# Closing loads of `wo` recut, two closing copies moved to ScalarE, and the load of `x` issued later

## The chip, the cores and the metric

The kernel runs on one core of a Trainium2 chip. A core has a matrix engine (TensorE, called PE in the profile, with its weight loads shown apart as PEld), three engines for element-wise work (VectorE, called DVE; ScalarE, called ACT; GpSimd, called POOL) and SyncE (SP), which here only issues transfers. Sixteen DMA engines carry data between HBM, the chip's large memory, and SBUF, the core's working memory. TensorE writes its results into PSUM, a small memory of eight banks, from which VectorE and ScalarE copy them out. The engines run at the same time and wait for one another through semaphores.

The metric is the device time of one execution in microseconds (us). A median of several executions is given, and beside it one further execution was taken by the hardware profiler; that one has a time of its own, and all durations of single instructions come from it.

## What is computed

One token (a row `x` of 1024 numbers) goes through an attention block and a two-layer MLP, and the results are added to `x`:

```python
xn = layernorm(x)
# attention on layernorm'ed x; 32 query heads, 4 key/value heads, last 4096 positions of the caches
q  = (xn @ wq) as 32 heads of 128
p  = softmax(q @ k.T * 128**-0.5)          # k, v: [4 heads, 4096, 128]
a  = (p @ v as 4096 numbers) @ wo          # wo: [4096, 1024]
# MLP on layernorm(xn)
h  = gelu(layernorm(xn) @ w1 + b1)         # w1: [1024, 3584]
m  = h @ w2 + b2                           # w2: [3584, 1024]
out = x + a + m                            # 1024 numbers
```

All inputs and the output are bf16. The weights and the used part of the caches are some 40 MB, each number of which is used once.

## The kernel before

The kernel is straight-line code: every instruction is written out in order for each engine, and waits on semaphores are set by hand. Each engine does its own list strictly in order.

**Loads.** All the large transfers go through SP's queue, in this order: `wq` (8 MB, into the SBUF buffer `WA`), two loads of keys (into `KT`), `w1` (7 MB, into `W1`), two loads of values (into `V`), then `w2` (7 MB, again into `WA`, issued once the product with `wq` is done, L298), then `wo` (8 MB, issued once the product with `w1` is done, L382 to L387). The weights are laid out so that each of the 128 partitions takes a run of consecutive rows; the 4096 rows of `wo` are 32 rows (of 1024 numbers, 2 KB) on each partition. The helper `load_rows` (L148) issues one transfer for each entry of a list of row counts, and each transfer has a semaphore of its own. `WO_CHUNKS` (L29) is that list for `wo`. Its first three entries, 28 rows, go into `W1`, whose weights have been used by then; the rest goes into `KT`, whose keys have been used by then.

ScalarE issues the three small loads: `x` and `b1` (L169, L170) after a wait for VectorE's third memset (`C["qbz"]`, L165), and `b2` (L245) after the first transpose of `x` (L241).

**GpSimd** builds constants from the start on: a matrix of ones, an identity, the selection matrix `SELQ` (L181 to L186, whose end is called `C["selq"]`), then masks and further selection matrices. SP's key loads wait for `C["selq"]` (L187).

**The front of the work.** `x` lands, VectorE transposes it (L241), then come sums on TensorE (L252), a square root on ScalarE (L256), and the normalised `XNTb` (L260); a second norm gives `YTb` (L277). TensorE waits for `wq` and multiplies (L289, name `"q"`). The keys are transposed on VectorE (L331), TensorE makes the scores (L345), softmax follows (L352 to L380), then the product with `w1` (L289 again, name `"h"`), the product with the values (L427), the GELU (L391 to L413, result `GT`) and the attention output `OT` (L448).

**The closing product.** The products with `w2` and with the first 28 rows of `wo` (`WO_BULK`, L30) go to one PSUM bank, bank 6: for each row two matmuls of 512 columns (`bulk`, L457 to L461), which leave one result row on partition 0 and one on partition 32. The last four rows of `wo` take another form: four matmuls of 256 columns each (L482), which leave their results in bank 7 on partitions 0, 32, 64 and 96, in the layout in which the output leaves. TensorE waits for the semaphore of each transfer of `wo` before its rows (L473). When the last of the 28 rows is done (`C["bulk"]`), VectorE copies the two result rows as four pieces of 256 numbers into `BULK` (L489 to L492), in that same layout. It then waits for the last matmul (`C["fin"]`), adds bank 7 and `BULK` (L495), and SP stores the result (L497).

Of the kernel before, what the change touches and what calls it, by code (L numbers as in the profile page):

```python
# [6 lines left out]
ACTF = mybir.ActivationFunctionType  # L7
AX = mybir.AxisListType

D = 1024  # L10
# [15 lines left out]
WQ_CHUNKS = [8]  # L26
W1_CHUNKS = [8]
W2_CHUNKS = [28]
WO_CHUNKS = [16, 8, 4, 2, 1, 1]  # L29
WO_BULK = 28  # L30


class Track:
# [11 lines left out]
def bass_parallel_sum__sliding_block_cached__mixer_channel_mlp__decode_kernel(  # L45
# [18 lines left out]
    pe, dve, act, pool, sp = nc.tensor, nc.vector, nc.scalar, nc.gpsimd, nc.sync  # L64

    def sems(name, n):
        return [nc.alloc_semaphore(f"{name}{i}") for i in range(n)]

    s_x, s_b1, s_b2, s_out = (nc.alloc_semaphore(n) for n in ("s_x", "s_b1", "s_b2", "s_out"))
# [3 lines left out]
    s_v = sems("s_v", NP)  # L73
    s_wo = sems("s_wo", len(WO_CHUNKS))
    s_w2 = sems("s_w2", len(W2_CHUNKS))

    PE = Track(nc, "S_PE")
    DVE = Track(nc, "S_DVE")
    ACT = Track(nc, "S_ACT")
    POOL = Track(nc, "S_POOL")  # L80

    def sb(name, shape, d):
        return nc.alloc_sbuf_tensor(name, shape, d)
# [3 lines left out]
    W1 = sb("W1", [128, KC * F], bf16)  # L87
    KT = sb("KT", [128, HKV * W], bf16)
# [7 lines left out]
    XB4 = sb("XB4", [128, 256], bf16)  # L96
    XT32 = sb("XT32", [128, 256], bf16)
    B1R = sb("B1R", [128, QW], bf16)
# [29 lines left out]
    OT = sb("OT", [128, 32], bf16)  # L128
    BULK = sb("BULK", [128, 256], f32)
    ORow = sb("ORow", [128, 256], bf16)  # L130
    PS = nc.alloc_psum_tensor("PS", [128, 8 * 512], f32)

    def bank(b, lo=0, n=512):
        return PS[:, b * 512 + lo: b * 512 + lo + n]

    x_rows = A_x.rearrange("b s (a n) -> (b s a) n", a=4)
    b2_rows = B_b2.rearrange("(a n) -> a n", a=4)
    b1_rows = B_b1.rearrange("(a n) -> a n", a=4)
# [3 lines left out]
    wo_p = A_wo.rearrange("(p j) n -> p j n", j=32)  # L142
    out_rows = out.rearrange("b s (a n) -> (b s a) n", a=4)

    C = {}


    def load_rows(dst, src, chunks, width, semaphores, first=0, c0=0, off=0):  # L148
        for j, n in enumerate(chunks):
            sp.dma_start(  # L150
                dst[:, off + c0 * width: off + (c0 + n) * width].rearrange("p (c n) -> p c n", c=n),
                src[:, first + c0: first + c0 + n, :],
            ).then_inc(semaphores[j], 16)
            c0 += n

    load_rows(WA, wq_p, WQ_CHUNKS, NQ, s_wq)
    def d(ins):
        return DVE.mark(ins)

    def dw():  # L160
        dve.wait_ge(DVE.sem, DVE.cnt)
# [2 lines left out]
    C["b1z"] = d(dve.memset(B1R[:, :], 0.0))  # L164
    C["qbz"] = d(dve.memset(QB[:, :], 0.0))  # L165

    with nc.allow_non_contiguous_dma(reason="small loads"):
        act.wait_ge(DVE.sem, C["qbz"])
        act.dma_start(XB4[0:128:32, :], x_rows).then_inc(s_x, 16)  # L169
        act.dma_start(B1R[0:128:32, :], b1_rows).then_inc(s_b1, 16)  # L170

    def p(ins):
        n = POOL.mark(ins)
        pool.wait_ge(POOL.sem, n)
        return n
# [6 lines left out]
    for q in range(4):  # L182
        ap = SELQ[32 * q:32 * q + 32, q * 128:(q + 1) * 128].rearrange("p (a j) -> p a j", a=4)
        p(pool.affine_select(out=ap, in_=ap, pattern=[[0, 4], [-1, 32]], compare_op=ALU.not_equal,
                             fill=1.0, base=0, channel_multiplier=1))
    C["selq"] = POOL.cnt  # L186
    sp.wait_ge(POOL.sem, C["selq"])  # L187
    for G in range(NP):
        sp.dma_start(
# [120 lines left out]
    for a in range(4):  # L310
        last = pe.matmul(bank(6, 16 + 32 * a, 32), lhsT=SELQ[:, a * 128:(a + 1) * 128], rhs=TQ[:, 0:1024:32],  # L311
                         start=True, stop=True)
# [14 lines left out]
    for G in range(NP):  # L327
        dve.wait_ge(s_k[G], 16)
        for h in range(2):
            lo = G * PW + h * W  # L330
# [8 lines left out]
    for G in range(NP):  # L339
        kg = KT[:, G * PW:(G + 1) * PW].rearrange("p (b c i) -> p c b i", b=PB, c=4)  # L340
        for nb in range(4):
            if nb % 2 == 0:
                pe.wait_ge(DVE.sem, C["kt"][2 * G + nb // 2])
            for c in range(4):
                last = pe.matmul(bank(nb), lhsT=QB[:, G * 512 + c * 128:G * 512 + (c + 1) * 128],  # L345
                                 rhs=kg[:, c, 16 * nb:16 * nb + 16, :], start=False,
                                 stop=(G == NP - 1 and c == 3))
# [29 lines left out]
        out=LR[:, :],  # L377
        in_=PS[0:1, 2 * 512 + 192:2 * 512 + 320].rearrange("o (a m) -> o m a", a=4), axis=AX.X, op=ALU.add))
    dw()
    C["rr"] = d(dve.reciprocal(  # L380
        out=RR4[:, :].rearrange("o (q m) -> o q m", q=4), in_=LR[:, :].unsqueeze(1).to_broadcast([1, 4, 32])))
# [1 line left out]

    wide_product(W1, W1_CHUNKS, F, s_w1, YTb, QW // 2, [4, 5], "h")
    sp.wait_ge(PE.sem, C["h"])
    load_rows(W1, wo_p, WO_CHUNKS[:3], D, s_wo[:3])
    load_rows(KT, wo_p, WO_CHUNKS[3:], D, s_wo[3:], first=WO_BULK)  # L387

    dve.wait_ge(PE.sem, C["h"])
    dve.wait_ge(s_b1, 16)  # L390
# [1 line left out]
        out=HW32[:, :].rearrange("p (b n) -> p b n", b=2),  # L392
# [32 lines left out]
    for t in range(32):  # L425
        q = t % 2
        last = pe.matmul(PS[64 * q:64 * q + 64, 3 * 512:4 * 512], lhsT=PT[:, t * 64:(t + 1) * 64], rhs=vb[:, t],  # L427
                         start=(t < 2), stop=(t >= 30))
# [7 lines left out]
        out=OM[:, :].rearrange("p (g d) -> p g d", g=HKV), in0=bank(3).rearrange("p (g d) -> p g d", g=HKV),  # L436
# [6 lines left out]
    for dq in range(4):  # L443
        last = pe.matmul(bank(2, 352, 32), lhsT=E4[:, dq * 128:(dq + 1) * 128],  # L444
                         rhs=ON[:, dq * 32:(dq + 1) * 32], start=(dq == 0), stop=(dq == 3))
# [11 lines left out]
    def bulk(weights, vec, c, lo, first, last):  # L457
        for q in range(2):
            ins = pe.matmul(PS[32 * q:32 * q + 1, 6 * 512:7 * 512], lhsT=vec[:, c:c + 1],  # L459
                            rhs=weights[:, lo + q * 512: lo + (q + 1) * 512], start=first, stop=last)  # L460
        return ins  # L461

    pe.wait_ge(DVE.sem, C["GT"])
    c = 0
# [6 lines left out]
    c = 0  # L471
    for j, n in enumerate(WO_CHUNKS):
        pe.wait_ge(s_wo[j], 16)  # L473
        for _ in range(n):
            if c < WO_BULK:
                last = bulk(W1, OT, c, c * D, False, c == WO_BULK - 1)
                if c == WO_BULK - 1:
                    C["bulk"] = PE.mark(last)
            else:
                for a in range(4):  # L480
                    lo = (c - WO_BULK) * D + a * 256
                    last = pe.matmul(PS[32 * a:32 * a + 32, 7 * 512:7 * 512 + 256],  # L482
                                     lhsT=OT[:, c:c + 1].to_broadcast([128, 32]), rhs=KT[:, lo:lo + 256],
                                     start=False, stop=(c == 31))
            c += 1
    C["fin"] = PE.mark(last)

    dve.wait_ge(PE.sem, C["bulk"])
    for a in range(4):  # L489
        q = a // 2  # L490
        lo = 6 * 512 + (a % 2) * 256
        d(dve.tensor_copy(BULK[32 * a:32 * a + 1, :], PS[32 * q:32 * q + 1, lo:lo + 256]))  # L492
    dw()
    dve.wait_ge(PE.sem, C["fin"])
    C["out"] = d(dve.tensor_tensor(out=ORow[:, :], in0=bank(7, 0, 256), in1=BULK[:, :], op=ALU.add))  # L495
# [33 lines left out]
```

## Time and profile before

| | |
|---|---|
| median of 3 runs | 101.97 us (101.0 to 102.63) |
| the profiled execution's own time | 100.91 us |
| its span, first to last instruction | 99.6 us |
| mean granted TensorE clock in it | 0.846 |
| TensorE busy | 48.4 us (49%), weight loads 19.3 us |
| VectorE busy | 38.8 us (39%) |
| ScalarE busy | 6.6 us (7%) |
| GpSimd busy | 9.6 us (10%) |
| read from HBM | 39.86 MB, 400 GB/s over the span |

The span is what the instructions show; 1.31 us of the profiled execution's time lie outside it. In the groups of the page, a line reads: line of the kernel, engine, operation, what it writes and reads, shapes and count, then busy time, mean duration in ns, and the idle time before it with the engine or transfer that ended it. In the timeline the two numbers ahead of a line are its start and its length in us. "SPq" and "ACTq" are the parts of SP and ScalarE that issue transfers. The row "PEclk" gives the granted clock of TensorE in tenths, the row "DMA" the busy share of the sixteen DMA engines in tenths, each over 40 equal slices of the span. The trace behind the page also holds a record of each DMA packet: queue, start, duration and bytes.

### The profile page before, as it was taken

What the parts mean: (1) busy time and instruction counts of PE and PEld (TensorE: products, weight loads), DVE (VectorE), ACT (ScalarE), POOL (GpSimd) and SP (SyncE); (2) the same over time, 40 slices, a digit from 0 to 9 for tenths busy, and PEclk for the clock granted to TensorE, in tenths of its full rate; (3) what the DMA queues carried; (4) which work ended last, traced back from release to release, by engine and by line L of the source; (5) the groups of instructions that cost most, each with busy time, mean ns of one, the idle gap of its engine ahead of it and who ended that gap; (6) DMA issues with size and microseconds to landing.
All of it is one profiled execution on the core that took longest, in us unless ns stands there. A gap on an engine that the chain in (4) does not pass through costs nothing.

```text
span 99.6 us, 859 instructions
## 1 busy us (share of the span) xinstructions
PE 48.4 (49%) x350; PEld 19.3 (19%) x350; DVE 38.8 (39%) x50; ACT 6.6 (7%) x11; POOL 9.6 (10%) x40
## 2 busy tenths in 40 slices
PE   0000220008973419756071179990800899795760
PEld 0000220003321003112020133540700223241210
DVE  4000443000027999999918175498100000000052
ACT  0000236000022000000000620000000000000000
POOL 5777720000000000000000000000000000000000
PEclk9999999999999555599999755999555558999999
DMA  9199999939999889998699999999889999999920
GB/s 421 79 474 553 423 474 474 447 132 428 428 441 651 368 368 391 529 529 375 253 428 428 434 510 414 483 553 391 368 368 431 421 414 421 414 424 390 382 100 1
DMA packets 1906, 39.89 MB, mean 400 GB/s; under 512 B 224, under 2 KB 240, under 8 KB 624
## 3 DMA queue, kind: packets, MB, share of 16 engines
q1 hardware_dynamic: 1880, 39.85, 93.9%
q8 instruction: 2, 0.03, 0.1%
q10 hardware_dynamic: 24, 0.01, 0.0%
HBM read 39.86 MB, written 0.00 MB: 400 GB/s over the span
## 4 chain that ended last, share of the span: by engine, by line
DMA 52%; DVE 25%; PE 17%; ACT 2%; issue 1%; SPq 0%; DVEq 0%
DMA W<-in_A_wo_dram 30%; DMA WA<-in_A_wq_dram 22%; DVE KT L331 17%; PE PS L289 12%; DVE MX L352 2%; ACT WA L367 2%; PE PS L345 2%; DVE BULK L492 2%; DVE TQ L307 1%; PE PS L459 1%; DVE Q L302 1%; DVE QB L322 1%; SPq L150 0%; DVE ORow L495 0%; PE PS L311 0%
## 5 line engine op out<-in xcount | busy, mean ns | idle before, releaser
L331 DVE STREAM_TRANSPOSE KT<-KT 128x4096 bf16<-128x4096 bf16 x4 | 17.4, 4412 | 0.0
L345 PE MATMUL PS<-KT,QB 128*128 128x512 bf16 x32 | 9.7, 459 | 8.7 <-DVE KT L331 8.7
L459 PE MATMUL PS<-WA,GT 128*1 128x512 bf16 x56 | 9.0, 498 | 5.1 <-DMA WA<-in_B_w_dram 5.1
L492 DVE COPY BULK<-PS 1x256 f32<-1x256 f32 x4 | 1.7, 417 | 23.4 <-PE PS L459 23.3
L289 PE MATMUL PS<-WA,XNTb 128*32 128x512 bf16 x64 | 6.5, 592 | 7.9 <-DMA WA<-in_A_wq_dram 7.9
L459 PE MATMUL PS<-W,OT 128*1 128x512 bf16 x56 | 6.5, 378 | 2.5 <-DMA W<-in_A_wo_dram 2.5
L252 PE MATMUL PS<-XT,onesf 128*128 128x16 f32 x2 | 0.6, 386 | 11.7 <-DVE XT L249 11.7
L345 PEld LDWEIGHTS PS<-KT,QB 128*128 128x128 bf16 x32 | 3.3, 112 | 15.6 <-DVE KT L331 11.5
L302 DVE CAST Q<-PS 128x512 bf16<-128x512 f32 x1 | 0.7, 692 | 13.1 <-PE PS L289 13.1
L289 PE MATMUL PS<-W,YTb 128*32 128x448 bf16 x64 | 5.4, 525 | 0.0
L459 PEld LDWEIGHTS PS<-WA,GT 128*1 128x1 bf16 x56 | 2.9, 104 | 10.9 <-issue 9.3
L289 PEld LDWEIGHTS PS<-WA,XNTb 128*32 128x32 bf16 x64 | 2.4, 142 | 11.6 <-DMA WA<-in_A_wq_dram 8.0
L241 DVE STREAM_TRANSPOSE XT<-XB 128x256 bf16<-128x256 bf16 x1 | 0.6, 625 | 8.5 <-DMA XB<-in_A_x_dram 8.5
L427 PE MATMUL PS<-V,WA 128*64 128x512 bf16 x32 | 3.6, 380 | 0.0
L459 PEld LDWEIGHTS PS<-W,OT 128*1 128x1 bf16 x56 | 2.2, 83 | 6.9 <-DMA W<-in_A_wo_dram 2.8
L367 ACT ACTIVATE WA<-PS,NMB 128x2048 bf16<-128x2048 f32 x1 | 2.0, 1967 | 23.3 <-DVE NMB L365 23.3
L444 PE MATMUL PS<-ON,E 128*128 128x32 f32 x8 | 1.9, 404 | 2.8 <-DVE ON L439 2.8
L370 DVE STREAM_TRANSPOSE WA<-WA 128x2048 bf16<-128x2048 bf16 x1 | 2.3, 2312 | 2.1 <-ACT WA L367 2.1
L352 DVE TENSOR_REDUCE MX<-PS 128x1 f32<-128x2048 f32 x1 | 2.3, 2291 | 2.0 <-PE PS L345 2.0
L289 PEld LDWEIGHTS PS<-W,YTb 128*32 128x32 bf16 x64 | 2.2, 138 | 3.0 <-issue 2.8
L252 PEld LDWEIGHTS PS<-XT,onesf 128*128 128x128 f32 x2 | 0.5, 312 | 11.7 <-DVE XT L249 11.7
L215 POOL TENSOR_SCALAR_AFFINE_SELECT E<-E 32x512 f32<-32x512 f32 x4 | 2.5, 629 | 0.6
(87 smaller groups left out, 37.3 us busy)
## 6 DMA issues: line engine op xcount, KB each, us to landing
W<-in_B_w_dram SPq DMA_DIRECT2D x1, 7168.0 KB, 45.2
WA<-in_B_w_dram SPq DMA_DIRECT2D x1, 7168.0 KB, 48.1
KT<-in_A_k_cache_dram SPq DMA_DIRECT2D x2, 2048.0 KB, 25.6
V<-in_A_v_cache_dram SPq DMA_DIRECT2D x2, 2048.0 KB, 51.6
W<-in_A_wo_dram SPq DMA_DIRECT2D x1, 4096.0 KB, 23.5
W<-in_A_wo_dram SPq DMA_DIRECT2D x1, 2048.0 KB, 28.0
W<-in_A_wo_dram SPq DMA_DIRECT2D x1, 1024.0 KB, 30.0
KT<-in_A_wo_dram SPq DMA_DIRECT2D x1, 512.0 KB, 30.8
```

Of the source, the lines that this page charges most:

```text
L215: p(pool.affine_select(out=ap, in_=ap, pattern=[[1, 4], [-1, 128]], compare_op=ALU.not_equal, fill=1.0, base=0, channel_multiplier=4))
L289: last = pe.matmul(PS[32 * a:32 * a + 32, banks[b] * 512: banks[b] * 512 + n], lhsT=vec[:, k:k + 1].to_broadcast([128, 32]), rhs=weights[: ...
L302: d(dve.tensor_copy(Q4[:, 0:512], bank(4)))
L331: C["kt"].append(d(dve.transpose(KT[:, lo:lo + W], KT[:, lo:lo + W])))
L345: last = pe.matmul(bank(nb), lhsT=QB[:, G * 512 + c * 128:G * 512 + (c + 1) * 128], rhs=kg[:, c, 16 * nb:16 * nb + 16, :], start=False, st ...
L352: C["mx"] = d(dve.tensor_reduce(out=MX[:, :], in_=PS[:, 0:2048], axis=AX.X, op=ALU.max))
L367: C["exp"] = ACT.mark(act.activation(out=Pb, in_=PS[:, 0:2048], func=ACTF.Exp, bias=NMB[:, 0:1], scale=SCALE, accum_out=RS[:, 0:1]))
L370: C["PT"] = d(dve.transpose(PT, Pb))
L427: last = pe.matmul(PS[64 * q:64 * q + 64, 3 * 512:4 * 512], lhsT=PT[:, t * 64:(t + 1) * 64], rhs=vb[:, t], start=(t < 2), stop=(t >= 30))
L444: last = pe.matmul(bank(2, 352, 32), lhsT=E4[:, dq * 128:(dq + 1) * 128], rhs=ON[:, dq * 32:(dq + 1) * 32], start=(dq == 0), stop=(dq == 3))
L459: ins = pe.matmul(PS[32 * q:32 * q + 1, 6 * 512:7 * 512], lhsT=vec[:, c:c + 1], rhs=weights[:, lo + q * 512: lo + (q + 1) * 512], start=fi ...
L492: d(dve.tensor_copy(BULK[32 * a:32 * a + 1, :], PS[32 * q:32 * q + 1, lo:lo + 256]))
```

## The change

Three things are changed.

1. `wo` is loaded in five transfers of 16, 9, 4, 2 and 1 rows in place of six of 16, 8, 4, 2, 1 and 1. The first two (25 rows, `WO_W1`) go into `W1`, the last three into `KT`. `WO_BULK` is 29 in place of 28: one more row takes the two matmuls of 512 columns, one fewer the four of 256.
2. Of the four closing copies, VectorE keeps the two from partition 0 and ScalarE takes the two from partition 32. VectorE gets a wait for ScalarE's second copy ahead of the closing addition.
3. ScalarE's issue of `x` and `b1` is moved behind GpSimd's `SELQ` in the code and waits for `C["selq"]` as well as for `C["qbz"]`.

```diff
-WO_CHUNKS = [16, 8, 4, 2, 1, 1]
-WO_BULK = 28
+WO_CHUNKS = [16, 9, 4, 2, 1]
+WO_BULK = 29
+WO_W1 = 25
...
-    with nc.allow_non_contiguous_dma(reason="small loads"):
-        act.wait_ge(DVE.sem, C["qbz"])
-        act.dma_start(XB4[0:128:32, :], x_rows).then_inc(s_x, 16)
-        act.dma_start(B1R[0:128:32, :], b1_rows).then_inc(s_b1, 16)
...
     C["selq"] = POOL.cnt
+    with nc.allow_non_contiguous_dma(reason="small loads"):
+        act.wait_ge(POOL.sem, C["selq"])
+        act.wait_ge(DVE.sem, C["qbz"])
+        act.dma_start(XB4[0:128:32, :], x_rows).then_inc(s_x, 16)
+        act.dma_start(B1R[0:128:32, :], b1_rows).then_inc(s_b1, 16)
     sp.wait_ge(POOL.sem, C["selq"])
...
-    load_rows(W1, wo_p, WO_CHUNKS[:3], D, s_wo[:3])
-    load_rows(KT, wo_p, WO_CHUNKS[3:], D, s_wo[3:], first=WO_BULK)
+    load_rows(W1, wo_p, WO_CHUNKS[:2], D, s_wo[:2])
+    load_rows(KT, wo_p, WO_CHUNKS[2:], D, s_wo[2:], first=WO_W1)
...
             if c < WO_BULK:
-                last = bulk(W1, OT, c, c * D, False, c == WO_BULK - 1)
+                last = bulk(W1 if c < WO_W1 else KT, OT, c, (c if c < WO_W1 else c - WO_W1) * D, False,
+                            c == WO_BULK - 1)
...
-                    lo = (c - WO_BULK) * D + a * 256
+                    lo = (c - WO_W1) * D + a * 256
...
     dve.wait_ge(PE.sem, C["bulk"])
+    act.wait_ge(PE.sem, C["bulk"])
     for a in range(4):
         q = a // 2
         lo = 6 * 512 + (a % 2) * 256
-        d(dve.tensor_copy(BULK[32 * a:32 * a + 1, :], PS[32 * q:32 * q + 1, lo:lo + 256]))
+        if q == 0:
+            d(dve.tensor_copy(BULK[32 * a:32 * a + 1, :], PS[32 * q:32 * q + 1, lo:lo + 256]))
+        else:
+            C["bulk_a"] = ACT.mark(act.activation(out=BULK[32 * a:32 * a + 1, :],
+                                                  in_=PS[32 * q:32 * q + 1, lo:lo + 256], func=ACTF.Copy))
+    dve.wait_ge(ACT.sem, C["bulk_a"])
     dw()
     dve.wait_ge(PE.sem, C["fin"])
```

## The prediction

> **What bounds the kernel now.** I read the page first, for the share of the DMA engines and the queues:
>
> ```profile
> DMA  9199999939999889998699999999889999999920
> ...
> q8 instruction: 2, 0.03, 0.1%
> ```
>
> Transfers fill the span. The low digits (1, 3) are long packets booked in one slice; in the packet records the engines follow packet on packet from 1.82 us to 96.56 us. So a step ahead of 95 us counts only if it delays the issue of a transfer past its turn. The last such issues, those of `wo`, are over at 66.35 us, and the first packet of `wo` starts at 74.99: it stood in line. Only the head and the tail are free to move. So the tail, in the chain of work that ended last:
>
> ```profile
> 94.58 1.05 PE PS L459 x8
> ...
> 96.99 0.42 DVE BULK L492
> ...
> 97.45 0.04 issue
> 97.49 0.42 DVE ORow L495
> ```
>
> Four copies (95.65 to 97.41) release the addition. Beside them the timeline has the last row of `wo`:
>
> ```profile
> 97.07 0.29 PE L482 MATMUL PS<-KT,OT 128*32 128x256 bf16 x4 [0.33 <-DMA KT<-in_A_wo_dram]
> ```
>
> It ends at 97.36, so with 0.04 of issue the addition could start at 97.40: the copies hold it up by 0.09 us. Then busy shares by stretch; the last but one number is that of the DMA engines:
>
> ```profile
> 95.00:95.50 0.50, 0.50 (x6) 0.09 (x2) 0.00 (x0) 0.00 (x0) 0.00 (x0) 1.00 0.39 143
> 95.50:96.00 0.50, 0.26 (x10) 0.12 (x8) 0.35 (x1) 0.00 (x0) 0.00 (x0) 1.00 0.14 53
> ```
>
> At the end 0.14 is busy: two engines of sixteen. The packet records name the cause: the two "instruction" packets of q8 (46.52 to 47.51, 81.36 to 82.38) each held one engine for 1.0 us, and these two have been last at every landing since.
>
> **1. The loads of `wo`.** The bytes stay. Each engine serves 8 partitions: 8 packets per load and a closing one. Packet records: 2 KB 0.084 us, 4 KB 0.159, 8 KB 0.311, 16 KB 0.611, 32 KB 1.215, closing 0.009. Between 16 and 32 KB a further 2 KB cost 0.075, so the new 18 KB packet should take 0.686. Before: 8 x (1.215 + 0.611 + 0.311 + 0.159 + 2 x 0.084) = 19.71. After: 8 x (1.215 + 0.686 + 0.311 + 0.159 + 0.084) = 19.64. With one closing packet fewer: -0.08 us. Bounds: 0, and +0.6 if the 18 KB packets ran at the 2 KB packets' rate (0.041 ns per byte against 0.037, on 8 x 18432 bytes); I take the interpolation, because 56 KB packets, no power of two either, took 2.12 us, the same 0.037. SP's issue of one load (0.43 us) goes too, far ahead of its turn: nothing.
>
> The last matmuls then run from 97.07 - 0.08 = 96.99 to 97.28. Back from there by the old spacings (0.62 for one row, 1.27 for two), the four-row load, which now closes bank 6, frees TensorE at 95.10; eight matmuls take 1.05 as before, so bank 6 is done at 96.15 (before: 95.63). The nine rows ahead need 2.1 us (their 16 matmuls took 1.89) from about 92.65 on and are out of the way. That one row changes from the narrow to the wide form is hidden in TensorE's waits for `wo`.
>
> **2. The copies.** VectorE keeps two: from 96.17, 0.41 + 0.03 + 0.41, to 97.02. A copy of 1x256 by ScalarE is not in the trace. Nearest: 0.27 us (32x128) and 0.60 (128x512); by columns 256 lies at 0.38, which I take. Two end at about 96.96, beside VectorE's. Both are done before 97.28, so the new wait, behind which only the addition stands, costs nothing. At 0.27 nothing changes; at 0.60 ScalarE ends at 97.40, the addition starts at 97.46, and 0.03 is left of the gain. A table load (1.28 us at L273) would add another 0.8; but the Copy at L304 ran behind that load and the Exp at L367 behind a Copy, both without a further load, so it is left out.
>
> TensorE's last row then sets the addition: 97.28 + 0.04 = 97.32 in place of 97.49, **-0.17 us**. Late next is that landing itself; addition, store and its landing (2.1 us) only move along.
>
> **3. The issue of `x`.** The timeline:
>
> ```profile
> 2.14 1.07 ACTq L169 DMA_DIRECT2D XB<-in_A_x_dram  x1
> 2.53 1.64 POOL L184 TENSOR_SCALAR_AFFINE_SELECT SELQ<-SELQ 32x128 bf16<-32x128 bf16 x4
> ...
> 10.61 0.62 DVE L241 STREAM_TRANSPOSE XT<-XB 128x256 bf16<-128x256 bf16 x1 [8.50 <-DMA XB<-in_A_x_dram]
> ...
> 22.81 6.46 PE L289 MATMUL PS<-WA,XNTb 128*32 128x512 bf16 x64 [7.93 <-DMA WA<-in_A_wq_dram]
> ```
>
> `SELQ` ends at 4.17, so `x` (1.07) and `b1` (0.51) are issued some 2.05 us later, beside SP's issues (4.19 to 7.34). In the records the packets of `x` take turns with those of `wq`: 7.3 to 7.8, and their closing packets one `wq` packet (2.44) later, at 9.8 to 10.3. Later by 2.05 means one turn later: `x` lands at 13.0 instead of 10.6. Behind the waiting ScalarE stand `b1`, then `b2`, the table load and the square root; VectorE and TensorE wait for them. `XNTb` comes at 16.3 instead of 13.82; the product waits for `wq` until 22.81. Cover: 8.96 us. If `x` kept to the very last turn of `wq`, it landed by 22.7 and the product began 3.2 us late; that too is covered, by TensorE's 5.07 us of waiting for `w2` at 77.5. `b1` is read at 63.65, `b2` at 72.07. SP's loads only join a line that lasts to 21.6. So nothing is lost. A gain is bounded by the head: `wq`'s first sixteen packets took 3.05 us in the mean, the next ones 2.45, while `x` was being issued. If the issue of `x` were the cause, 0.6 would come back; a first packet must also fill the path, so I take 0 and keep -0.6 for the range.
>
> **Sum.** 100.91 - 0.17 = 100.74 for the profiled execution. The median of the runs lies 1.06 above it, so 101.97 - 0.17 = **101.8 us**. What a measurement of this kernel tells from no change is about 2%: 99.9 to 104.0.
>
> **Rivals.**
>
> *Slower: TensorE's clock falls in the tail.* The granted clock changes in steps of 3.41 us. Stretches of one step, PE's busy time first, then PEld, DVE, ACT, POOL, clock:
>
> ```profile
> 28.58:31.99 3.41, 1.25 (x18) 0.43 (x11) 2.07 (x3) 0.73 (x2) 0.00 (x0) 1.00 1.42 610
> 42.23:45.64 3.41, 1.42 (x8) 0.46 (x6) 3.41 (x2) 0.00 (x0) 0.00 (x0) 1.00 1.16 504
> 66.12:69.54 3.42, 1.35 (x14) 0.46 (x10) 2.89 (x10) 0.23 (x1) 0.00 (x0) 1.00 1.24 537
> 90.87:94.28 3.41, 1.89 (x16) 0.61 (x16) 0.00 (x0) 0.00 (x0) 0.00 (x0) 1.00 0.98 393
> ```
>
> After the first and third the clock fell to half, after the second it did not: the point lies near 1.4 us of work. The nine-row load stretches the wait before it from 1.18 to 1.78 us, so the emptiest step of the tail has 3.41 - 1.78 = 1.63 us of work instead of 1.89. At half clock a row takes 0.43 us (w2 from 77.5 on). From 93.4 on it would cost some 0.9 us against before; from 91 on the nine rows end at 96.5, the four at 98.2, the addition starts at 99.15: +1.7. That is 102.8 to 103.6. For it: the small margin. Against: 1.63 is above every step that lost the clock. The Trainium skill (TensorE: Matmul & The Clock Gate, Part 1) lets the clock fall only after an idle window of about 3.4 us; by that rule it would stay up and this rival be void. The trace disagrees: it fell after steps with 1.25 and 1.35 us of work.
>
> *Slower by less: both q8 packets on one engine*, or a third on one of the two: +1.0, 102.8. The program hardly changes in length, so little speaks for it.
>
> *A free head:* -0.6 beside the tail's gain: 101.2.
>
> *Each load has a price of its own.* From issue to first packet `wq` took 1.0 us; were that paid per load, one fewer gives 100.8. The last two loads landed 0.62 apart with 8 x 0.084 = 0.67 of packets: no room for it. The Trainium skill (DMA: Bandwidth & Descriptors, Anatomy of one DMA) gives about 2.0 us fixed per DMA on GpSimd's path; by that it would be 99.8, and the spacing of 0.62 disagrees.
>
> **Chances.** Forecast 0.55, clock 0.11, free head 0.10, q8 0.05, price per load 0.04; 0.15 stays for what one trace can't show, as three runs of one kernel lie 1.6% apart, 0.09 of it slower by over 2%, 0.06 faster. Slower by over 2%: that 0.09 and 0.04 of the clock's, where a high run adds to it. Faster: 0.06 and 0.02 from the head and the price per load. Within 2%: 0.79. The forecast's own range is 100.9 to 102.6, by the spread of the runs; with the free head below and the clock above, 100.3 to 103.4.
>
> **What would show it.** Right: the chain ends with TensorE's last row, not the copies; the last landing is 0.05 to 0.1 earlier; ScalarE's copies take about 0.38; `x` is transposed at 13.0 and the product still starts at 22.8. Wrong: a half clock behind 90 us, a table load before the copies, the two late engines gone or doubled, a first `wq` packet of 2.5 us.

## The result, and the profile after

| | before | after |
|---|---|---|
| median of 22 runs each | 101.11 us (100.82 to 102.96) | 101.72 us (101.21 to 102.72) |
| ratio of after to before, 95% interval | | 1.0065 (1.0039 to 1.0091) |
| the profiled execution's own time | 100.91 us | 101.21 us |
| its span | 99.6 us | 99.6 us |
| what lies outside its span | 1.3 us | 1.6 us |

The changed kernel is 0.65% slower. That is well inside the 2% of "no change", and its median lies inside the forecast range, but its sign is clear and it is not the forecast one. The two spans are equal to a tenth: what was lost isn't between the first and the last instruction.

Inside the span the change did nearly what its steps say. The closing part of the timeline of the changed kernel (start and length in us, engine, line):

```profile
96.17 0.77 ACT L498 ACTIVATE BULK<-PS 1x256 f32<-1x256 f32 x2 [28.42 <-PE PS L460]
96.17 0.86 DVE L496 COPY BULK<-PS 1x256 f32<-1x256 f32 x2 [23.57 <-PE PS L460]
...
96.96 0.29 PE L484 MATMUL PS<-KT,OT 128*32 128x256 bf16 x4 [0.23 <-DMA KT<-in_A_wo_dram]
97.40 0.42 DVE L503 TENSOR_TENSOR ORow<-PS,BULK 128x256 bf16<-128x256 f32 x1 [0.38 <-PE PS L484]
```

Both engines' copies are over at 97.03, the last row of `wo` starts 0.11 us earlier than before (96.96 against 97.07), and the addition 0.09 us earlier (97.40 against 97.49). The chain of work that ended last now goes through TensorE's last row and not through the copies:

```profile
65.66 31.26 DMA KT<-in_A_wo_dram
96.92 0.04 issue
96.96 0.32 PE PS L484 x4
97.28 0.03 issue
97.31 0.05 DVEq L502
97.36 0.04 issue
97.40 0.42 DVE ORow L503
```

At the front, `x` comes later and the product with `wq` still waits for its weights, as its bracket says:

```profile
12.74 0.63 DVE L242 STREAM_TRANSPOSE XT<-XB 128x256 bf16<-128x256 bf16 x1 [10.64 <-DMA XB<-in_A_x_dram]
...
23.03 6.46 PE L290 MATMUL PS<-WA,XNTb 128*32 128x512 bf16 x64 [6.00 <-DMA WA<-in_A_wq_dram]
```

So the experiments had to find where 0.6 us went that no line of the profile shows. Each execution has its own time and span; their difference is called "the time outside" below, and its shortest value in a kernel's runs is its steadiest number. For the changed kernel it is 1.61 us in 22 executions (median 1.71); for the kernel before, in 29 executions beside the first experiments, 1.21 us (median 1.28). The medians of the spans are 99.8 and 99.7 us. Of the 0.61 us between the medians of the times, some 0.4 thus lie outside the span and at most 0.1 inside (the medians of two parts need not add up to the median of the whole). The ratios below rest on 6 executions (the shared copies alone) to 13 of each kernel, and on 19 to 35 of the kernel before taken beside them.

### The profile page after: what moved, and what is told of

Its sections match the earlier page's. It is cut to its first block, busy times and chain, and to the rows that moved or that the text cites. A ratio compares the mean times of both kernels' runs of the same rounds, so it can differ in the third digit from the quotient of the medians.

```text
span 99.6 us, 855 instructions
## 1 busy us (share of the span) xinstructions
PE 46.8 (47%) x348; PEld 18.8 (19%) x348; DVE 38.0 (38%) x48; ACT 7.3 (7%) x13; POOL 9.6 (10%) x40
## 4 chain that ended last, share of the span: by engine, by line
DMA 54%; DVE 23%; PE 16%; ACT 2%; SPq 1%; issue 1%; DVEq 0%
DMA KT<-in_A_wo_dram 31%; DMA WA<-in_A_wq_dram 22%; DVE KT L332 18%; PE PS L290 12%; DVE MX L353 2%; ACT WA L368 2%; PE PS L346 2%; SPq L151 1%; DVE TQ L308 1%; DVE Q L303 1%; DVE QB L323 1%; DVE ORow L503 0%; PE PS L312 0%; PE PS L364 0%; PE PS L374 0%
## 5 line engine op out<-in xcount | busy, mean ns | idle before, releaser
L496 DVE COPY BULK<-PS 1x256 f32<-1x256 f32 x2 | 0.8, 414 | 23.6 <-PE PS L460 23.6
L460 PE MATMUL PS<-WA,GT 128*1 128x512 bf16 x56 | 7.5, 435 | 4.6 <-DMA WA<-in_B_w_dram 4.6
L460 PE MATMUL PS<-W,OT 128*1 128x512 bf16 x50 | 5.7, 379 | 4.2 <-DMA W<-in_A_wo_dram 4.2
L498 ACT ACTIVATE BULK<-PS 1x256 f32<-1x256 f32 x2 | 0.7, 372 | 28.4 <-PE PS L460 28.4
```

## Experiments

**One part at a time.** Four kernels, each the kernel before with one edit.

Part 2 alone, the two copies on ScalarE exactly as in the diff of the change:

> The kernel before with part 2 of the change alone: VectorE and ScalarE share the four closing copies; loads and the issue of x stay. Three theories on the 0.6 us that the changed kernel lost. Theory L (late ScalarE): ScalarE's last work moves from 67.5 us to some 96.5 us, and what the device still does on ScalarE at the end of a program comes later; it lies outside the span. L expects the time outside the span to rise from 1.31 us to about 1.65, and the median by 0.3 to 0.6 us. Theory X (late x): the loss comes from issuing x beside SP's issues; X expects no change here (within 0.15 us). Theory W (loads): the loss comes from the recut loads; no change here either.

Part 3 alone, the issue of `x` and `b1` behind `SELQ`:

> The kernel before with part 3 alone: x and b1 issued behind GpSimd's SELQ. X expects the median up by 0.3 to 0.6 us, most of it inside the span, by a slower start of wq (its landing at 22.99 us in the changed kernel, 22.77 before). L and W expect no change within 0.15 us and 1.31 us outside the span.

ScalarE only waits where the copies would stand:

```diff
     dve.wait_ge(PE.sem, C["bulk"])
...
+    act.wait_ge(PE.sem, C["bulk"])
     dw()
     dve.wait_ge(PE.sem, C["fin"])
```

> The kernel before with one wait added at the end of ScalarE's list: it waits for the end of bank 6 (95.6 us) and does nothing after it. No copy is moved, no other engine waits for it. L in its strict form (it matters only when ScalarE reaches the end of its list) expects the same loss as with the copies, 0.3 to 0.6 us, 1.65 us outside the span. If the loss comes from the copies themselves, or from X or W, the time is that of before within 0.15 us.

Part 1 without part 2, with bank 6 closed earlier so that VectorE's four copies are hidden:

```diff
-WO_CHUNKS = [16, 8, 4, 2, 1, 1]
-WO_BULK = 28
+WO_CHUNKS = [16, 9, 4, 2, 1]
+WO_BULK = 25
...
-    load_rows(W1, wo_p, WO_CHUNKS[:3], D, s_wo[:3])
-    load_rows(KT, wo_p, WO_CHUNKS[3:], D, s_wo[3:], first=WO_BULK)
+    load_rows(W1, wo_p, WO_CHUNKS[:2], D, s_wo[:2])
+    load_rows(KT, wo_p, WO_CHUNKS[2:], D, s_wo[2:], first=WO_BULK)
```

> The kernel before with wo in five loads of 16, 9, 4, 2 and 1 rows, but with 25 rows in bank 6 and 7 rows in the narrow form, so that VectorE's four copies (1.76 us) start at about 94.7 us and end at 96.5, ahead of the last landing; ScalarE and x as before. L and X expect 0.05 to 0.2 us less than before (one load less, last landing at 96.95 instead of 97.03, no copies in the way) and 1.31 us outside the span. W expects a loss of 0.3 to 0.6 us.

| kernel | ratio to before (95%) | time outside, shortest / median |
|---|---|---|
| shared copies alone | 1.0066 (1.0041 to 1.0091) | 1.61 / 1.66 us |
| late `x` alone | 1.0006 (0.9976 to 1.0037) | 1.21 / 1.25 |
| ScalarE waits, no copies | 1.0003 (0.9992 to 1.0014) | 1.23 / 1.26 |
| loads alone | 0.9984 (0.9957 to 1.0010) | 1.20 / 1.27 |

The whole loss comes with the shared copies, outside the span. X and W fall; so does L in its strict form, because ScalarE's list ended at 95.9 us without a loss.

**Is it ScalarE?** Four more, to see whether ScalarE's operation, their number or the end of its list matters. Two copies that nobody needs, put at three places:

```diff
+    act.wait_ge(PE.sem, C["bulk"])
+    act.wait_ge(POOL.sem, C["consts"])
+    for i in range(2):
+        ACT.mark(act.activation(out=SCR[0:1, i * 128:(i + 1) * 128], in_=identf[0:1, :], func=ACTF.Copy))
     dve.wait_ge(PE.sem, C["bulk"])
```

The first wait is for `C["bulk"]` in the late kernel and for `s_wo[0]` in the middle one; the early one has no such wait and stands behind the GELU's exponential.

> The kernel before, with two added ScalarE copies of 1x128 from a constant into a buffer that nobody reads, behind the end of bank 6 (95.6 us), so that they end at about 96.2. VectorE keeps its four copies and waits for nothing new. The loss of the shared copies was 0.40 us outside the span (shortest 1.61 us, against 1.21 before), and a bare wait at that place cost nothing. Four theories. E (operation late): any operation that ScalarE executes late brings the 0.40; expects 1.61 us outside and +0.4 to 0.6 in the median. N (count): two more ScalarE instructions bring it wherever they stand; the same here. T (end of the list): what counts is when ScalarE's list ends; the bare wait ended at 95.9 and was early enough, the copies at 96.6 not; expects a part, 0 to 0.2. S (sharing): it takes VectorE's wait for ScalarE, or both reading bank 6; expects no change.

> The same two added copies, but behind the landing of the first load of wo (87.2 us), so that they end near 87.7, some 12 us ahead of the end. E expects the loss to shrink or to be gone, depending on how long before the end it still counts; N expects the full 0.40 us outside the span; T and S expect no change.

> The same two added copies directly behind the exponential of the GELU (67.5 us), where ScalarE's list ended before. N expects the full 0.40 us outside the span and +0.4 to 0.6 in the median; E, T and S expect the time of before within 0.15 us.

The fourth has one bare wait at the end of ScalarE's list, `act.wait_ge(DVE.sem, C["out"])`:

> The kernel before with one bare wait at the end of ScalarE's list, now for the closing addition (97.9 us), later than the shared copies ended (96.6 to 96.9). No operation is added. T expects a loss of at least 0.40 us outside the span, more than with the copies since the list ends a further 1 us later; E, N and S expect no change (within 0.15 us).

| kernel | ratio to before (95%) | time outside, shortest / median |
|---|---|---|
| two added copies, late | 0.9989 (0.9965 to 1.0012) | 1.21 / 1.27 us |
| in the middle | 0.9986 (0.9965 to 1.0008) | 1.23 / 1.27 |
| early | 0.9993 (0.9963 to 1.0022) | 1.22 / 1.27 |
| bare wait for the addition | 1.0010 (0.9979 to 1.0041) | 1.21 / 1.29 |

None loses. My theory that ScalarE's late work is the cause was wrong in all its forms (E, N, T). What is left of the edit is what it takes from VectorE, and the two engines' sharing.

**VectorE's list.** The expectations count "entries": the operations of VectorE, as the page counts them, and its seven separate waits (57 is 50 operations, 55 is 48).

Two copies left out, nothing for ScalarE (`for a in range(2)` in place of `range(4)`):

> The kernel before in which VectorE makes only the two copies from partition 0; the two from partition 32 are left out altogether (half of the closing sums are then missing from the output), and ScalarE does nothing new. The loss of the shared copies (0.40 us outside the span) came neither from a late ScalarE operation nor from two more of them in its list. Theories left. V (VectorE's list): VectorE's list is two operations shorter, and what runs around the program depends on that; expects 1.61 us outside the span here and the median up by 0.4. S (sharing): it takes ScalarE's reading of PSUM and VectorE's wait for it; expects 1.21 us outside and the time of before or up to 0.1 less. A (ScalarE's list of exactly this length): expects the time of before.

Both engines copy; VectorE's list keeps its length:

```diff
+    act.wait_ge(PE.sem, C["bulk"])
+    for a in (2, 3):
+        lo = 6 * 512 + (a % 2) * 256
+        C["bulk_a"] = ACT.mark(act.activation(out=SCR[32 * a:32 * a + 1, :],
+                                              in_=PS[32:33, lo:lo + 256], func=ACTF.Copy))
     for a in range(4):
         q = a // 2
         lo = 6 * 512 + (a % 2) * 256
+        if a == 2:
+            dve.wait_ge(ACT.sem, C["bulk_a"])
         d(dve.tensor_copy(BULK[32 * a:32 * a + 1, :], PS[32 * q:32 * q + 1, lo:lo + 256]))
```

> VectorE makes all four copies as before, and ScalarE makes its two as well, out of the same PSUM row but into a buffer that nobody reads; VectorE waits for ScalarE ahead of its third copy. So ScalarE reads PSUM late and VectorE waits for it, but VectorE's list is not shorter. S expects 1.61 us outside the span and the median up by 0.4 to 0.6; V expects the time of before within 0.15 us and 1.21 us outside. A expects the loss as well.

The shared copies, with VectorE's list filled up:

```diff
+    dve.wait_ge(POOL.sem, C["consts"])
+    for i in range(2):
+        d(dve.tensor_copy(SCR[0:1, i * 128:(i + 1) * 128], identf[0:1, :]))
     dve.wait_ge(ACT.sem, C["bulk_a"])
```

> The shared copies of the changed kernel (loads and x as before), and VectorE gets two further copies of 1x128 from a constant into a buffer that nobody reads, behind its own two and ahead of its wait for ScalarE; they end before the last row of wo lands. VectorE's list is then as long as before the change. V expects the loss to be gone: 1.21 us outside the span, median as before within 0.15 us. S and A expect it to stay: 1.61 us and +0.4 to 0.6.

The shared copies, with ScalarE's list filled up by `act.wait_ge(POOL.sem, C["consts"])`:

> The shared copies of the changed kernel (loads and x as before), and ScalarE gets one more wait, for GpSimd's constants, which were done at 13 us; its list is then as long as in the kernels with two added late copies, which lost nothing. A expects the loss to be gone (1.21 us outside the span); S and V expect it to stay (1.61 us, +0.4 to 0.6 in the median).

| kernel | VectorE operations | ratio to before (95%) | time outside, shortest / median |
|---|---|---|---|
| two copies left out | 48 | 1.0028 (0.9999 to 1.0058) | 1.60 / 1.66 us |
| both engines copy | 50 | 0.9992 (0.9957 to 1.0027) | 1.24 / 1.30 |
| shared, VectorE filled up | 50 | 0.9985 (0.9959 to 1.0011) | 1.22 / 1.29 |
| shared, ScalarE filled up | 48 | 1.0023 (0.9995 to 1.0050) | 1.63 / 1.68 |

S falls, A falls, V stands: the kernel without a single new ScalarE operation loses the 0.40 us, and the shared copies lose nothing once VectorE's list is filled up. The intervals of the two losing kernels' ratios just take in 1, since the times outside scatter upwards in both kernels compared; their shortest and median values don't overlap with those of any kernel with 50 operations.

**Length or place?** The changed kernel with two tiny memsets at the start of VectorE's list, 94 us ahead of the copies:

```diff
     C["qbz"] = d(dve.memset(QB[:, :], 0.0))
+    for i in range(2):
+        d(dve.memset(PAD[:, 8 * i:8 * i + 8], 0.0))
```

> The changed kernel as it is, and two memsets of 1x8 into a buffer that nobody reads, at the start of VectorE's list (2.1 us), where VectorE then idles for 10 us. VectorE's list is again as long as before the change (57 entries in the trace, 55 in the changed kernel). Theory V, length: what counts is how many instructions VectorE's list has, wherever they stand; expects the 0.40 us outside the span to go (1.21 instead of 1.61) and the median 0.0 to 0.2 us under the kernel before. Theory P, place: it takes the closing copies on VectorE, or VectorE at work near the end; expects the loss to stay (1.61 us, +0.4 to 0.6).

And the kernel before with one closing copy left out, or with one, two, four or eight such memsets added:

> The kernel before without VectorE's fourth closing copy (a quarter of the closing sums is then missing from the output): 56 entries. V, length, as a step between 55 and 57: either 1.21 or 1.61 us outside the span, nothing between, and it tells on which side 56 lies. V, as a price per missing instruction: 1.41 us. P: between the two, or as with two copies left out (1.61).

> The kernel before with one memset of 1x8 into a buffer that nobody reads, at the start of VectorE's list: 58 entries. V as a step (shorter than 56 or 57 entries loses): 1.21 us outside, the time of before within 0.15 us. V as a pattern that repeats (an odd or even count, or the place of the list's end within a block): 1.61 us and +0.4 are possible here. P: the time of before.

> The same with two such memsets: 59 entries. V as a step and P: the time of before within 0.15 us, 1.21 us outside. V as a pattern of two or four: 1.61 us is possible here or one entry earlier.

> The kernel before with four added memsets of 1x8 at the start of VectorE's list: 61 entries, four more than the 57 of before. The shortest times outside the span so far, by entries: 55: 1.60, 56: 1.64, 57: 1.20, 58: 1.36, 59: 1.42 us. Theory R4, a pattern that repeats every four entries: 1.2 us outside, the time of before. Theory R8, every eight entries: above 1.4 us. Theory G, growing with each entry past 57: 1.5 to 1.6 us.

> The same with eight added memsets: 65 entries. R4 and R8: 1.2 us outside, the time of before. G: 1.7 us or more, the median up by 0.5 or more.

| kernel | VectorE operations | ratio to before (95%) | time outside, shortest / median | median span |
|---|---|---|---|---|
| changed kernel, two memsets | 50 | 1.0007 (0.9978 to 1.0036) | 1.23 / 1.29 us | 99.8 us |
| one copy left out | 49 | 1.0041 (1.0015 to 1.0068) | 1.64 / 1.86 | 99.6 |
| one memset added | 51 | 1.0026 (1.0008 to 1.0044) | 1.36 / 1.41 | 99.9 |
| two added | 52 | 1.0022 (0.9995 to 1.0049) | 1.42 / 1.59 | 99.7 |
| four added | 54 | 1.0103 (1.0075 to 1.0130) | 1.21 / 1.26 | 100.9 |
| eight added | 58 | 1.0025 (0.9982 to 1.0069) | 1.28 / 1.55 | 99.8 |

The two memsets bring the changed kernel back to the time of before: it is the length of VectorE's list, wherever the instructions stand, and P falls. One copy left out gives 1.64, not 1.41: a missing instruction has no price of its own. The page's first part has busy time, share and count for each engine; first the changed kernel:

```profile
PE 46.8 (47%) x348; PEld 18.8 (19%) x348; DVE 38.0 (38%) x48; ACT 7.3 (7%) x13; POOL 9.6 (10%) x40
```

then the same with the memsets, where VectorE (DVE) has 50 operations in the same 38.0 us:

```profile
PE 48.3 (49%) x348; PEld 19.2 (19%) x348; DVE 38.0 (38%) x50; ACT 7.3 (7%) x13; POOL 9.7 (10%) x40
```

The copies of the two kernels take the same time and start within 0.03 us (this is the timeline of the kernel with the memsets):

```profile
96.20 0.77 ACT L501 ACTIVATE BULK<-PS 1x256 f32<-1x256 f32 x2 [28.74 <-PE PS L463]
96.20 0.86 DVE L499 COPY BULK<-PS 1x256 f32<-1x256 f32 x2 [23.90 <-PE PS L463]
...
97.45 0.42 DVE L506 TENSOR_TENSOR ORow<-PS,BULK 128x256 bf16<-128x256 f32 x1 [0.39 <-PE PS L487]
```

With fewer than 50 operations the time outside is longer, but so it is with 51 and 52, by less, which neither the step nor the repeating pattern had forecast; with 54 it is short and the span is 1.1 us longer, in every run. G and R8, which expected 1.4 us and more outside there, fall with that, and R4, which expected the time of before; eight added memsets leave a shortest value of 1.28 and a median of 1.55 us outside. Four added memsets show one way in which the length costs time. That kernel's queues on the page have a line that the kernel before has not, a packet on q14:

```profile
q8 instruction: 2, 0.03, 0.1%
q10 hardware_dynamic: 24, 0.01, 0.0%
q14 instruction: 1, 0.01, 0.0%
```

and SP's own waits have 2.0 us for the output where the kernel before and the changed kernel have 1.0; first the kernel before, then the one with four memsets:

```profile
SPq L498 <- DMA out_dram<-ORow: 1.0, 1, 1.0
```

```profile
SPq L500 <- DVE ORow L498: 32.5, 1, 32.5
...
SPq L501 <- DMA out_dram<-ORow: 2.0, 1, 2.0
```

In the packet records this is a block of 8 KB of instructions, from 99.40 to 99.88 us. One of the four 512-byte packets of the output goes at 99.87, as the block ends, while the other three went by 99.43; its landing comes at 100.75 instead of 99.78. The records kept here name no DMA engine, so it is inferred from these times that block and packet shared one. The time of such a block goes with the length of VectorE's list: with eight memsets it is at 71.19 us, far from the end and without harm to the span; with four at 99.40; with two at 101.06 and with one at 101.68, behind the last instruction. The longer the list, the earlier in it the block's turn comes. With 48 to 50 operations no q14 packet of 8 KB stands in the records behind the first instruction; but the latest record of any run starts 1.80 us behind the last instruction, and a fetch later than that would not be seen.

So shown is this: the loss follows the length of VectorE's list, and a block of VectorE's instructions, whose turn moves with that length, is fetched close to the end of the program, where it costs 1.0 us in one case. That the same fetch, or the wait for it, makes the 0.40 us of the lists with 48 and 49 is only argued; their records show no packet for it, and it stays open why 50 is better than 51.

The records give one more hint, on the scatter of the time outside. In four of the twenty profiled executions it is 0.6 to 1.0 us above the median of its kernel (two added copies late, one, four and eight memsets added); in the sixteen others by 0.3 at most. Just these four have an instruction packet of 16 KB on q8 that starts 1.3 to 1.4 us behind the last instruction. Which of the two causes the other isn't shown, as a longer execution may only leave more time for the record. A third q8 packet near the end of the span, at 96.3 to 97.5 us, does not go with the loss: seven kernels have it, six of them with 50 operations, and four of the five kernels with 48 or 49 do not.

No kernel here beats the one before by more than its interval. The lowest ratio is that of the loads alone, with 25 rows in bank 6, 0.9984 (0.9957 to 1.0010); two useless copies in the middle have 0.9986, so it can't be told from no gain.

## Why the prediction was wrong

**The step that failed is the sum.** It took the span's gain of 0.17 us and carried what lies outside the span over unchanged, as if it were a constant of the device: forecast -0.17 us, measured +0.61. The time outside rose by 0.40 us, because part 2 makes VectorE's list two operations shorter. No rival had that: all of them looked for a cost inside the span, and the step on ScalarE's copies priced the two that ScalarE gets and not what the two that VectorE loses could change besides their time. The Trainium skill (Runtime: NRT & Kernel Launch, Instruction fetch mechanics) says that an engine's instructions are fetched in blocks by transfers of their own, and calls the cost of crossing a block's end mostly hidden. The trace agrees with the first, as the packets on q8 and q14 show, and not with the second here: 1.0 us where the block met the output.

**The base was off too.** The median of three runs, 101.97, was high; 22 runs give 101.11. The forecast of 101.8 lies close to the measured 101.72 by the accident of two errors, a base 0.86 too high and a change 0.8 too low.

**The loads held.** Forecast: 18 KB packets of 0.686 us, the last matmuls from 96.99, the four-row load at 95.10, the copies from 96.17. Measured: 0.690 in the packet records, 96.96, 95.10 and 96.17.

**The copies were right in size, their worth was not.** ScalarE's took 0.372 us each (0.38 forecast), both engines were done at 97.03, and there was no table load. But the gain of 0.17 was 0.09. The prediction let the addition follow the last matmul by 0.04 us, which it took from the chain. In the kernel before it follows by 0.12 (97.37 to 97.49), and by the same 0.12 in two kernels whose copies are over 0.7 and 0.9 us before the last matmul ends: the loads alone, whose lines are these, and the two copies left out.

```profile
94.90 1.76 DVE L492 COPY BULK<-PS 1x256 f32<-1x256 f32 x4 [24.59 <-PE PS L459]
...
97.10 0.29 PE L482 MATMUL PS<-KT,OT 128*32 128x256 bf16 x4 [0.23 <-DMA KT<-in_A_wo_dram]
97.52 0.42 DVE L495 TENSOR_TENSOR ORow<-PS,BULK 128x256 bf16<-128x256 f32 x1 [0.86 <-PE PS L482]
```

So the copies had held up nothing, although the chain names them. And the new wait, which was to cost nothing, cost 0.03: in the five kernels in which VectorE waits for ScalarE directly ahead of the addition the gap is 0.15 us, and VectorE's wait instruction, which waits for two semaphores there, takes 0.05 us (DVEq L502 in the chain above). With one semaphore to wait for it took 0.02 before:

```profile
97.42 0.02 DVEq L494
```

The last matmul came 0.11 earlier (0.08 forecast), less these 0.03: that is the 0.09.

**The issue of `x` held in what it costs.** It was transposed 2.1 us later (12.74; forecast 13.0), and alone it made 1.0006. The product with `wq` began at 23.03 instead of 22.81, but with `x` late alone it began at 22.88, and in the kernels with `x` early anywhere from 22.67 to 23.25. The free head fell: the first sixteen packets of `wq` took 3.05 us in the mean although `x` was issued only from 4.19 us on.

**The clock did not fall** in the tail of the changed kernel's profiled execution. The stretch that was to be the emptiest has 1.68 us of work (forecast 1.63):

```profile
90.87:94.28 3.41, 1.68 (x16) 0.70 (x18) 0.00 (x0) 0.00 (x0) 0.00 (x0) 1.00 0.98 407
```

But in this execution the clock's steps lie elsewhere: it rose at 80.00, and steps of 3.41 us from there give an emptier one that the prediction hadn't seen. After it the clock stayed up as well:

```profile
83.41:86.83 3.42, 1.42 (x14) 0.39 (x10) 0.00 (x0) 0.00 (x0) 0.00 (x0) 1.00 0.94 404
86.83:90.24 3.41, 3.05 (x30) 1.29 (x32) 0.00 (x0) 0.00 (x0) 0.00 (x0) 1.00 1.01 432
```

So far as these runs show, that was luck: in the kernel with the loads alone, after a step with 1.43 us of work the next one ran at half clock, in its profiled execution:

```profile
84.27:87.68 3.41, 1.43 (x15) 0.47 (x12) 0.00 (x0) 0.00 (x0) 0.00 (x0) 1.00 0.89 382
87.68:91.10 3.42, 3.42 (x20) 1.06 (x16) 0.00 (x0) 0.00 (x0) 0.00 (x0) 0.51 0.98 416
```

It cost nothing there, since TensorE caught up before the nine rows were finished.

Nor was 1.63 us a safe margin: in the kernel with the shared copies alone the clock fell after a step with 1.70 us of work (95.13 to 98.54), where it cost nothing, as the last matmul had ended in it.

**The two late DMA engines** stayed two: 0.10 to 0.12 of the sixteen were busy from 95.5 to 96.5 us. **A price per load** was not there: one load fewer with a price of 1.0 us would have given a ratio of 0.990, and the loads alone have 0.9984 (0.9957 to 1.0010).

## What to carry to other kernels

When a profile ends all in its place and the time is longer, subtract the span from each execution's time and compare the rest: here it separated two kernels whose medians three runs couldn't. Once the tail is tuned to tenths of a microsecond, moving two small operations from one engine to another can cost more through the length of an engine's list than it gains, so repeat the edit with the list filled up (or made longer) by tiny operations in an idle place before a verdict on the edit itself. And a copy that ends last in the chain is worth only what the next event leaves: take the gap from that event to its consumer from a place where it is really the releaser.

## What the runs showed of the hardware that was not expected

- The time outside the span is about 1.2 us at its shortest for all kernels with 50 VectorE operations (1.20 to 1.24 in ten kernels, 1.20 to 1.25 in the kernel before) and 1.60 to 1.64 for those with 48 and 49; ScalarE's list, longer by up to three entries, changed nothing in it.
- A block of 8 KB of instructions on q14 took 0.48 us beside the output (0.32 to 0.51 in the kernels with one, two and eight memsets); a 512-byte packet of the output went 0.47 us after the last of the other three and landed 0.97 us after them.
- TensorE's granted clock fell to half after a step of 3.41 us with 1.43 us of matmul work in it (the loads alone), and of 1.70 (the shared copies alone), while it stayed up after one with 1.42 (the kernel before, the changed kernel): the busy time of a step alone doesn't decide it.
- VectorE's wait instruction ahead of the addition took 0.02 us where it waited for one semaphore and 0.05 where it waited for two; the addition followed the end of the last matmul by 0.12 and 0.15 us.
